# The first batch's product with v in the whole array with a column of ones, and an earlier pooling of q

## The chip, the cores and the metric

The kernel runs on one core of a Trainium2 chip. The metric is the device time of one execution in microseconds; it is the median of several runs. Five engines work side by side, each through its own queue of instructions in order: TensorE (PE in the rows: matrix products; its weight loads are PEld), VectorE (DVE), ScalarE (ACT), GpSimd (POOL), and SyncE (SP), which here issues all transfers (DMA).

## What is computed

```python
# attention: q, k, v are (batch 4, heads 8, 1152 positions, 64)
q_pool = q.reshape(B, H, S // 2, 2, D).mean(axis=3)          # 576 pooled queries
scores = scale * np.matmul(q_pool, k.transpose(0, 1, 3, 2))
scores = scores - np.max(scores, axis=-1, keepdims=True)
attn = np.exp(scores)
attn = attn / (np.sum(attn, axis=-1, keepdims=True) + 1e-09)
attn_out = np.matmul(attn, v)                                # to (2304 tokens, 512)
# two layers follow, (2304 x 512) by w_in (512 x 2048) and w_out (2048 x 512):
h = x @ w_in;  x = (h - np.tanh(h)) @ w_out                  # first layer
h = x @ w_in2; r = np.maximum(h, 0); x = (s*r*r + b) @ w_out2  # second layer
```

The weights of the layers arrive as 64-bit floats in two 32-bit words each, and are turned into pairs of 32-bit numbers on the chip.

## The kernel before

**Heads and tiles.** The 32 heads are worked off in 16 pairs (n = 0 to 15, four pairs for each of the four batches; the pair's heads are j = 0 and 1). One head has 9 tiles t of 128 keys. For a tile, `scores` makes the scores of 128 keys by 576 queries in two halves g of 288 queries, each by two products (L352 and L353), and ScalarE takes their exponential into a buffer pf (L354). The tile then waits in the list `pend` for its product with v.

**The product with v (tile pv).** `batch` takes three tiles at a time. v of a tile is 128 keys by 64, so that the product has 64 rows; the two halves g of the queries are put on the upper and the lower 64 rows of one PSUM tile, that is on two column tiles of the array that work side by side (L421, written 128*64 in the rows). Every product in plain 32 bits is two instructions in the trace (and one row in the order of instructions below); a head has 9 x 2 x 2 = 36 in the trace.

**The sum of a head's exponentials (tile su).** In the first batch (`plain`, n < 4) and for the very last head, `sum_plain` makes it on TensorE too: a product of 32 columns of ones with each pf (L387, 128*32), four column tiles side by side, again 36 in the trace for a head; after the head, ScalarE copies the result (sx, L394) and one product with `spread` (L396, tile pts) spreads it over 128 rows. From the second batch on, GpSimd adds up the pf of a head (`add`, L408, tile acc) and `total` makes one sum of them at the head's end (L434). `end` inverts the sum (tile ri, VectorE, L453); `store` multiplies it into the head's result (tile xv, copied from pv by L444), splits it on ScalarE and GpSimd (tile xo, L460), and `put` transfers it to DRAM (L464).

**Preparation.** `prep(n)` makes a pair's operands: it adds neighbouring q (tile qr, L265, on GpSimd for all pairs but the first), transposes q and k on TensorE (ptq L271, ptk L287), and makes the largest score of each query by a separate product (ptm, L312 to L316) that VectorE reduces (mp, L317; 27 a pair). VectorE and GpSimd also convert the first layer's weights in steps of seven instructions (tiles raw, t, w; L195 to L210), four steps in each pair of the first batch; a step reads raw, which a transfer fills (L178, L181), two steps ahead.

**Order.** The program is written by a clock of ticks, four for a tile. `prep(n + 2)` starts in the second head of pair n, at tile 9 - LEAD // 4, and goes on after so many ticks as its `yield`s say. Within TensorE's row of instructions a scheduler then orders by priority; `batch` is given a priority AHEAD = 400 and `prep`'s transposes SOON = 40. From pair 5 on, `fill` puts products of the first layer's first five slices for the batch before (tiles h, y: L487, L500) between the tiles; in the first pair of a batch (n = 4, 8, 12) there are none.

In PSUM, pv and su have one buffer each, pp (for ptm, ptq, ptk, pts) three, and the scores three.

Of the kernel before, what the change touches and what calls it, by code (L numbers as in the profile page):

```python
# [9 lines left out]
F32 = mybir.dt.float32  # L10
F32R = mybir.dt.float32r
I32 = mybir.dt.int32
AF = mybir.ActivationFunctionType
# [5 lines left out]
P = 128  # L19
# [5 lines left out]
LAG = 3  # L25
# [4 lines left out]
LAST_STEPS = 4  # L30


LEAD = 20
GAP = 30
GAP1 = 12
MAXSTEP = 2
# [20 lines left out]
def attention_moe_moe_kernel(  # L57
# [60 lines left out]
    for i in range(4):  # L118
        g = i % 2
        dve.memset(spread[32 * i:32 * i + 1, g * D:(g + 1) * D], 1.0)  # L120
    sb2 = cp.tile([P, 2], F32, name="sb2")

    NBH = B * 2
# [13 lines left out]
    def later(k, fn):  # L137
        queue.append((clock[0] + k, fn))
# [91 lines left out]
    kl = pp.tile([P, S], F32R, name="kl")  # L230
    qls = [pp.tile([P, SQ], F32R, name=f"ql{i}") for i in range(2)]
    cs = [pp.tile([NQS + 1 - j, P], F32R, name=f"c{j}") for j in range(2)]
    vos = [ap.tile([P, NKT, D], F32, name=f"vo{i}") for i in range(2)]
    U2 = [ap.tile([D + 1, SQ], F32R, name=f"U2_{j}") for j in range(2)]
    for j in range(2):
        dve.memset(f32(T2[j][D:D + 1, :]), 1.0)
# [15 lines left out]
    def v_of(n, j):  # L252
        b, hp = pairs[n]
        return v[b, 2 * hp + j].rearrange("(p t) d -> p t d", t=NKT)

    def prep(n):
# [5 lines left out]
        for j in range(2):  # L262
            eng = dve if n == 0 else pool
            with tc.issue_after(added[0].ins) if n > 1 else ExitStack():
                eng.tensor_add(qrs[0][:, :, j * D:(j + 1) * D], qrs[j][:, :, 0:D], qrs[j][:, :, D:2 * D])  # L265
        yield 4
        for g in range(2):
            with tc.high_priority(offset=SOON):
                pt = psP.tile([P, KB], F32, tag="pp", name=f"ptq{n}_{g}")
# [58 lines left out]
    def prep_head(n, j):  # L328

        ql = qls[n % 2]  # L330
        T1, U1 = ops[n]
        with tc.issue_after(moved[0].ins) if moved[0] else ExitStack():
            dma(out=f32(U2[j][0:D, :]), in_=f32(ql[j * D:(j + 1) * D, :]))
            dma(out=f32(T2[j][0:D, :]), in_=f32(T1[j][j * D:(j + 1) * D, :]))
            dma(out=vos[j], in_=v_of(n, j))
        yield 1
        while (n, j) not in maxes:
            yield 1
        u = U2[j][D:D + 1]
        q0 = j * QH  # L340
        dma(out=f32(u[:, q0:q0 + NQS * P].rearrange("o (a t) -> o a t", t=P)), in_=f32(cs[j][0:NQS, :]))
        q0 = (1 - j) * NQS * P
        dma(out=f32(u[:, q0:q0 + QH]), in_=f32(cs[0][NQS:NQS + 1, j * QH:(j + 1) * QH]))
        ready.add((n, j))

    def scores(n, j, t):
        T1, U1 = ops[n]
        pf = ap.tile([P, SQ], F32, tag="pf", name=f"pf{n}_{j}_{t}", bufs=PFB)
        for g in range(2):
            sl = slice(g * HB, (g + 1) * HB)  # L350
            ps = psS.tile([P, HB], F32, tag="s", name=f"s{n}_{j}_{t}_{g}")
            last[0] = mm(ps, T1[j][:, t * P:(t + 1) * P], U1[j][:, sl], start=True, stop=False)  # L352
            last[0] = mm(ps, T2[j][:, t * P:(t + 1) * P], U2[j][:, sl], start=False, stop=True)  # L353
            act(pf[:, sl], ps, AF.Exp, scale=SCALE)  # L354
            yield
        pend.append((n, j, t, pf))
        if plain(n, j):
            fresh.append((n, j, t, pf))
            return
        r = [t in x for x in GROUPS].index(True)  # L360
        if t == GROUPS[r][0]:
            accs[n, j, r] = pf
        else:
            later(SUM, lambda: add(n, j, t, r, pf))
        if t == NKT - 1:
            later(SUM, lambda: due.append((n, j)))

    def plain(n, j):

        return n < NPAIR or (n, j) == (len(pairs) - 1, 1)  # L370

    fresh = []
    sums = {}
# [29 lines left out]
    def add(n, j, t, r, pf):  # L403
# [3 lines left out]
            accs[n, j, r] = ap.tile([P, SQ], F32, tag="acc", name=f"acc{n}_{j}_{r}", bufs=4)  # L407
        added[0] = pool.tensor_add(accs[n, j, r], old, pf)  # L408

    def batch():  # L410


        todo = [pend.popleft() for _ in range(BATCH)]
        n, j, t, _ = todo[0]
        if t == 0:
            pvt[n, j] = psV.tile([P, HB], F32, tag="pv", name=f"pv{n}_{j}")
        po = pvt[n, j]
        with tc.high_priority(offset=AHEAD), tc.issue_after(last[0].ins):
            for i, (_, _, u, pf) in enumerate(reversed(todo)):
                for g in (1, 0):  # L420
                    mm(po[g * D:(g + 1) * D], vos[j][:, u], pf[:, g * HB:(g + 1) * HB],  # L421
                       start=(t == 0 and i == 0), stop=(u == NKT - BATCH))
            total()
            if plain(n, j):
                sum_plain(n, j, t)
        if t == NKT - BATCH:
            later(0, lambda: finish_head(n, j))

    def total():
        for n, j in due:  # L430
            su = psV.tile([P, HB], F32, tag="su", name=f"su{n}_{j}")
            for r in range(2):
                for g in (1, 0):
                    mm(su[g * D:(g + 1) * D], ones, accs[n, j, r][:, g * HB:(g + 1) * HB],  # L434
                       start=(r == 0), stop=(r == 1))
            later(0, lambda: end(n, j, su))
        due.clear()
# [109 lines left out]
    def tick():  # L547

        clock[0] += 1
        due = [x for x in queue if x[0] <= clock[0]]  # L550
        queue[:] = [x for x in queue if x[0] > clock[0]]
        for _, fn in due:
            fn()
        for p in list(preps):
            if p[1] <= clock[0]:
                try:
                    p[1] = clock[0] + next(p[0])
                except StopIteration:
                    preps.remove(p)
        if done[0] < total_ns - HOLD_NS:  # L560
            fill(MOE_NS / 4)
# [10 lines left out]
    for n in range(len(pairs)):  # L572
        b, hp = pairs[n]
        if n == 0:
            add_prep(1)
        for j in range(2):
            for t in range(NKT):
                if j == 1 and t == NKT - LEAD // 4 and n + 2 < len(pairs):
                    add_prep(n + 2)
                if t == LAG + 1:  # L580
                    if j == 1 and n + 1 < len(pairs):
                        preps.append([prep_head(n + 1, 0), clock[0]])
                    if j == 0 and n > 0:
                        preps.append([prep_head(n, 1), clock[0]])
                if hp == 1 and j == 0 and t == 0 and b > 0:
                    while moe:
                        fill(1000)
                    moe.extend(sweep1(b - 1, g) for g in range(2))
                while (n, j) not in ready:
                    tick()  # L590
                for _ in scores(n, j, t):
                    tick()
                tick()
                if len(pend) > BATCH:
                    batch()
                tick()
                if (n, j, t) in early1:
                    w1gen.step()
                if n == len(pairs) - 1 and (n, 1) in ready:
                    if FW not in slots:  # L600
                        pctx.close()
                        wpc = ctx.enter_context(tc.tile_pool(name="wc", bufs=1, reuse_waits="tile"))
                        new_slots(wpc, range(FW, FA))
                    w1gen.step()
# [192 lines left out]
```

## Time and profile before

| | us |
|---|---|
| median of 3 runs (lowest, highest) | 1429.94 (1429.66, 1430.97) |
| the profiled execution | 1429.16 |
| its span, from the first to the last instruction | 1427.4 |
| TensorE busy in the span | 1359.7 |
| VectorE busy | 865.0 |
| ScalarE busy | 559.6 |
| GpSimd busy | 385.5 |

The attention takes about the first 680 us, the first batch of it about the first 190. A busy TensorE is counted from an instruction's start to its modelled end, and instructions overlap: one that has been issued and waits behind another counts too. Times in the rows are microseconds from the span's start.

### The profile page before, as it was taken

To read this page: it belongs to the slowest core of one execution; us is meant where nothing else is said; L and a number is where in the kernel's file an instruction comes from. 1 tells how busy PE (TensorE), PEld (TensorE's weight loads), DVE (VectorE), ACT (ScalarE), POOL (GpSimd) and SP (SyncE) were. 2 spreads that over 40 slices of the span, in tenths; PEclk is the share of its full clock that TensorE was granted. 3 is DMA by queue.
4 is the path that set the end of the run, shared out by engine and by line. 5 is a ranking of instruction groups with operands and counts; after the bars stand their busy time and mean duration, and the time that the engine had idled before them with its cause. 6 is when DMAs were issued, how large, how long until landed. Compare 5 with 4: busy or idle time off the path is not lost.

```text
span 1427.4 us, 23107 instructions
## 1 busy us (share of the span) xinstructions
PE 1359.7 (95%) x8670; PEld 1157.2 (81%) x8670; DVE 865.0 (61%) x1640; ACT 559.6 (39%) x1360; POOL 385.5 (27%) x311
## 2 busy tenths in 40 slices
PE   5999898999999999998989998999999999999998
PEld 3666666777777777776989997999899989898997
DVE  7877785667566664759796399844963232323232
ACT  2544445555455544544332233333332222323232
POOL 1212136565556645654220033100210000000000
PEclk9999999999999999999999999999999999999999
DMA  8756655563546555344776134744602020201000
GB/s 196 172 145 160 163 135 139 127 170 92 149 111 164 128 145 143 88 109 139 236 237 220 34 132 158 230 133 147 206 30 67 0 67 0 67 23 44 1 23 23
DMA packets 157647, 169.62 MB, mean 119 GB/s; under 512 B 52064, under 2 KB 130016, under 8 KB 157536
## 3 DMA queue, kind: packets, MB, share of 16 engines
q1 hardware_dynamic: 157536, 168.15, 42.8%
q8 instruction: 68, 1.11, 0.3%
q14 instruction: 43, 0.35, 0.1%
HBM read 101.98 MB, written 30.67 MB: 93 GB/s over the span
## 4 chain that ended last, share of the span: by engine, by line
PE 72%; DVE 16%; DMA 5%; POOL 3%; issue 3%; ACT 1%; SPq 1%; DVEq 0%; POOLq 0%; ACTq 0%
PE h L662 19%; PE o L735 14%; PE pv L421 9%; PE ptm L316 5%; PE y L673 5%; PE s L352 4%; PE s L353 4%; PE y L500 3%; PE h L487 2%; DVE t L199 2%; DMA raw<-in_moe_w_out_dram 2%; DVE t L197 2%; DVE mp L317 2%; DVE t L195 2%; POOL acc L408 2%
## 5 line engine op out<-in xcount | busy, mean ns | idle before, releaser
L662 PE MATMUL h<-xx,w 128*128 128x288 f32 (+1 forms) x2328 | 388.1, 316 | 1.7 <-DVE thb L514 1.7
L662 PEld LDWEIGHTS h<-xx,w 128*128 128x128 f32 x2328 | 365.1, 189 | 11.0 <-DVE thb L514 2.6
L317 DVE TENSOR_REDUCE mp<-ptm 128x1 f32<-128x384 f32 x432 | 225.2, 549 | 128.7 <-PE ptm L316 118.9
L354 ACT ACTIVATE pf<-s 128x288 f32<-128x288 f32 x576 | 220.8, 410 | 125.1 <-PE s L353 117.6
L210 POOL TENSOR_TENSOR w<-t,w 128x512 fp32r<-128x512 f32 (+1 forms) x82 | 98.0, 1195 | 381.4 <-ACT w L209 281.5
L673 PE MATMUL y<-ghb,w 128*128 128x288 f32 x784 | 174.5, 297 | 11.8 <-DVE yr L681 7.8
L408 POOL TENSOR_TENSOR acc<-acc,pf 128x576 f32<-128x576 f32 x115 | 166.3, 1446 | 64.8 <-ACT pf L354 60.0
L735 PE MATMUL o<-w,g2h 128*128 128x512 f32 x576 | 180.6, 395 | 0.0
L352 PE MATMUL s<-U,T 128*128 128x288 f32 x576 | 177.2, 314 | 0.6
L353 PE MATMUL s<-U,T 65*128 65x288 f32 x576 | 173.4, 309 | 1.1 <-DMA U<-c 1.1
L421 PE MATMUL pv<-pf,vo 128*64 128x288 f32 x1152 | 165.0, 423 | 0.0
L316 PE MATMUL ptm<-T,U 128*128 128x384 f32 x384 | 141.6, 387 | 16.6 <-DVE mp L317 10.8
L755 DVE SCALAR_TENSOR_TENSOR r<-r,sb 128x384 f32<-128x384 f32 x96 | 60.1, 626 | 140.7 <-ACT r L754 140.7
L673 PEld LDWEIGHTS y<-ghb,w 128*128 128x128 f32 x784 | 132.7, 190 | 13.5 <-DVE yr L681 8.9
L760 DVE SCALAR_TENSOR_TENSOR g2l<-r,sb,g2h 128x384 fp32r<-128x384 f32 x96 | 59.5, 620 | 111.1 <-ACT g2h L759 111.0
L421 PEld LDWEIGHTS pv<-pf,vo 128*64 128x64 f32 x1152 | 75.6, 139 | 59.6 <-ACT pf L354 10.6
L352 PEld LDWEIGHTS s<-U,T 128*128 128x128 f32 x576 | 111.6, 194 | 14.4 <-ACT pf L354 6.8
L735 PEld LDWEIGHTS o<-w,g2h 128*128 128x128 f32 x576 | 107.3, 188 | 18.0
L673 PE MATMUL y<-glb,w 128*128 128x288 f32 x392 | 117.0, 298 | 4.8 <-DVE glb L518 4.7
L353 PEld LDWEIGHTS s<-U,T 65*128 65x128 f32 x576 | 111.6, 194 | 5.9 <-issue 4.5
L735 PE MATMUL o<-w,g2l 128*128 128x512 f32 x288 | 114.1, 396 | 0.0
L759 ACT ACTIVATE g2h<-r,sb 128x384 fp32r<-128x384 f32 x96 | 59.5, 620 | 125.4 <-PE o L735 110.1
(78 smaller groups left out, 1747.6 us busy)
## 6 DMA issues: line engine op xcount, KB each, us to landing
xx<-x1d SPq DMA_DIRECT2D x80, 288.0 KB, 4.9
T<-T SPq DMA_DIRECT2D x48, 288.0 KB, 4.7
raw<-in_moe_w_in_dram SPq DMA_DIRECT2D x23, 512.0 KB, 3.7
raw<-in_moe_w_out_dram SPq DMA_DIRECT2D x23, 512.0 KB, 4.2
qr<-in_q_dram SPq DMA_DIRECT2D x32, 288.0 KB, 3.2
kr<-in_k_dram SPq DMA_DIRECT2D x32, 288.0 KB, 4.4
T<-kl SPq DMA_DIRECT2D x32, 288.0 KB, 4.2
vo<-in_v_dram SPq DMA_DIRECT2D x32, 288.0 KB, 5.0
```

What stands on the lines that cost most here:

```text
L210: added[0] = pool.tensor_sub(w[:, 2 * i + 1, cols], x, f32(w[:, 2 * i, cols]))
L316: mm(pt, Uz[j][:, q0:q0 + P], T1[j][:, kk], start=True, stop=True)
L317: dve.reduce_max(mp[:, s, i:i + 1], pt, axis=AX.X)
L352: last[0] = mm(ps, T1[j][:, t * P:(t + 1) * P], U1[j][:, sl], start=True, stop=False)
L353: last[0] = mm(ps, T2[j][:, t * P:(t + 1) * P], U2[j][:, sl], start=False, stop=True)
L354: act(pf[:, sl], ps, AF.Exp, scale=SCALE)
L408: added[0] = pool.tensor_add(accs[n, j, r], old, pf)
L421: mm(po[g * D:(g + 1) * D], vos[j][:, u], pf[:, g * HB:(g + 1) * HB], start=(t == 0 and i == 0), stop=(u == NKT - BATCH))
L662: mm(ps[:, :n], w[:, a, c * P:(c + 1) * P], xx[:, c, x, 0:n], start=(i == 0 and c == 0), stop=(i == 2 and c == NDC - 1))
L673: mm(ys[i][c], w[:, a, c * P:(c + 1) * P], x, start=(f == fa and r == 0), stop=(f == fb - 1 and r == 2))
L735: mm(ys[i][r], x[:, r * P:(r + 1) * P], w[:, a], start=(f == 0 and n == 0), stop=(f == NFC - 1 and n == 2))
L755: dve.scalar_tensor_tensor(out=r, in0=r, scalar=sb2[:, 0:1], in1=r, op0=ALU.mult, op1=ALU.mult)
```

## The change

For the pairs of the first batch, v gets a 65th column of ones. The product of a tile and a half g is then 65 rows: 64 of the result and one that is the sum of the exponentials. The halves go to two PSUM tiles, which take the buffers pv and su, with the whole array for each; they are issued tile by tile, three tiles behind the scores, without the priority of `batch`. At the head's end ScalarE copies two sum rows and two results, and two products with `rows` (65 by 128, zero but for half a row of ones) spread the sums. All later pairs keep the column tiles of 64. LEAD goes from 20 to 32 ticks, and for n > 1 `prep` leaves 16 ticks in place of 4 between the addition of q and its transposes, so that only the addition moves, by three tiles.

```diff
-LEAD = 20
+LEAD = 32
...
+    rows = []
+    for g in range(2):
+        row = fp.tile([D + 1, P], F32, name=f"row{g}")
+        dve.memset(row, 0.0)
+        dve.memset(row[D:D + 1, g * D:(g + 1) * D], 1.0)
+        rows.append(row)
+    srow = fp.tile([D + 1, 2, HB], F32, name="srow")
+    dve.memset(srow, 0.0)
...
-    vos = [ap.tile([P, NKT, D], F32, name=f"vo{i}") for i in range(2)]
+    vos = [ap.tile([P, NKT, D + 1], F32, name=f"vo{i}") for i in range(2)]
+    for vo in vos:
+        dve.memset(vo[:, :, D:D + 1], 1.0)
...
-        yield 4
+        yield 4 if n < 2 else 16
...
-            dma(out=vos[j], in_=v_of(n, j))
+            dma(out=vos[j][:, :, 0:D], in_=v_of(n, j))
...
         pend.append((n, j, t, pf))
+        if n < NPAIR:
+            return
         if plain(n, j):
...
-        return n < NPAIR or (n, j) == (len(pairs) - 1, 1)
+        return (n, j) == (len(pairs) - 1, 1)
...
+    def single():
+
+        n, j, t, pf = pend.popleft()
+        if t == 0:
+            pvt[n, j] = [psV.tile([P, HB], F32, tag=x, name=f"{x}{n}_{j}") for x in ("pv", "su")]
+        po = pvt[n, j]
+        for g in range(2):
+            mm(po[g][0:D + 1], vos[j][:, t], pf[:, g * HB:(g + 1) * HB],
+               start=(t == 0), stop=(t == NKT - 1))
+            yield
+        if t == NKT - 1:
+            later(0, lambda: finish_single(n, j))
+
+    def finish_single(n, j):
+        xv = xvs[n, j] = fp.tile([P, HB], F32, tag="xv", name=f"xv{n}_{j}", bufs=3)
+        po = pvt.pop((n, j))
+        for g in range(2):
+            act(srow[D:D + 1, g], po[g][D:D + 1], AF.Copy)
+            act(xv[g * D:(g + 1) * D], po[g][0:D], AF.Copy)
+
+        def total():
+            pt = psP.tile([P, KB], F32, tag="pp", name=f"pts{n}_{j}")
+            for g in range(2):
+                mm(pt[:, :HB], rows[g], srow[:, g], start=(g == 0), stop=(g == 1))
+            end(n, j, pt[:, :HB])
+
+        later(2, total)
...
-                tick()
-                if len(pend) > BATCH:
-                    batch()
-                tick()
+                if pend[0][0] < NPAIR:
+                    if len(pend) > LAG:
+                        for _ in single():
+                            tick()
+                    else:
+                        tick()
+                        tick()
+                else:
+                    tick()
+                    if len(pend) > BATCH:
+                        batch()
+                    tick()
```

**TensorE's row in the first batch.** The first rows are of before, pair 1, first head, around its second batch of three tiles: the last scores, one sum ahead, six products with v, the other sums, and then the products for VectorE's maxima. In a row stand the line, the tile written, the tiles read, and the size.

```order
L353 MATMUL s_0_6_1_930<-U_0_163,T_0_139 128x288
L387 MATMUL su_0_943<-pf_0_0_776,ones 32x288
L421 MATMUL pv_0_878<-pf_0_5_909,vo_161 64x288 x2
L421 MATMUL pv_0_878<-pf_0_4_885,vo_161 64x288 x2
L421 MATMUL pv_0_878<-pf_0_3_867,vo_161 64x288 x2
L387 MATMUL su_0_943<-pf_0_0_776,ones 32x288
L387 MATMUL su_0_943<-pf_0_1_821,ones 32x288 x2
L387 MATMUL su_0_943<-pf_0_2_838,ones 32x288 x2
L387 MATMUL su_0_943<-pf_0_3_867,ones 32x288 x2
L387 MATMUL su_0_943<-pf_0_4_885,ones 32x288 x2
L387 MATMUL su_0_943<-pf_0_5_909,ones 32x288 x2
L321 MATMUL ptc_1_848<-ident,m_1_675 4x128
```

The same head in the changed kernel (L430 is the product with the column of ones, L327 the product for the maxima, L363 and L364 the scores):

```order
L363 MATMUL s_0_6_1_907<-U_1_0_157,T_1_0_151 128x288
L364 MATMUL s_0_6_1_907<-U_0_173,T_0_147 128x288
L430 MATMUL pv_0_845<-pf_0_3_829,vo_169 65x288
L327 MATMUL ptm_0_0_1_912<-T_2_0_153,U_2_0_159 128x384
L430 MATMUL su_0_846<-pf_0_3_829,vo_169 65x288
L363 MATMUL s_0_7_0_925<-U_1_0_157,T_1_0_151 128x288
L364 MATMUL s_0_7_0_925<-U_0_173,T_0_147 128x288
L327 MATMUL ptm_0_0_2_931<-T_2_0_153,U_2_0_159 128x384
L363 MATMUL s_0_7_1_934<-U_1_0_157,T_1_0_151 128x288
L364 MATMUL s_0_7_1_934<-U_0_173,T_0_147 128x288
L430 MATMUL pv_0_845<-pf_0_4_856,vo_169 65x288
```

What stood in one block of 18 products now stands as single products between the scores and the maxima.

**VectorE's row at the same head.** Before, around the conversion of weight slice 0's second half (raw_0_1; L195 to L207), with the maxima mp around it:

```order
L317 TENSOR_REDUCE mp_0_925<-ptm_0_2_1_1008 128x1
L195 TENSOR_SCALAR t_0_1_0_1359<-raw_0_1_0_1291 128x256
L197 SCALAR_TENSOR_TENSOR t_0_1_0_1359<-raw_0_1_0_1291,t_0_1_0_1359 128x256
L199 SCALAR_TENSOR_TENSOR t_0_1_0_1359<-raw_0_1_0_1291,t_0_1_0_1359 128x256
L202 TENSOR_SCALAR raw_0_1_0_1291<-raw_0_1_0_1291 128x256
L204 SCALAR_TENSOR_TENSOR t_0_1_0_1359<-raw_0_1_0_1291,t_0_1_0_1359 128x256
L207 CAST w_121<-t_0_1_0_1359 128x256
L195 TENSOR_SCALAR t_0_1_1_1414<-raw_0_1_1_1334 128x256
L197 SCALAR_TENSOR_TENSOR t_0_1_1_1414<-raw_0_1_1_1334,t_0_1_1_1414 128x256
L317 TENSOR_REDUCE mp_0_925<-ptm_0_2_2_1038 128x1
```

In the changed kernel, the steps of the same head's conversions (L204 to L216; L328 is the maximum):

```order
L328 TENSOR_REDUCE mp_0_902<-ptm_0_2_0_967 128x1
L204 TENSOR_SCALAR t_4_0_0_1204<-raw_4_0_0_889 128x256
L206 SCALAR_TENSOR_TENSOR t_4_0_0_1204<-raw_4_0_0_889,t_4_0_0_1204 128x256
L328 TENSOR_REDUCE mp_0_902<-ptm_0_2_1_975 128x1
L208 SCALAR_TENSOR_TENSOR t_4_0_0_1204<-raw_4_0_0_889,t_4_0_0_1204 128x256
L328 TENSOR_REDUCE mp_0_902<-ptm_0_2_2_984 128x1
L211 TENSOR_SCALAR raw_4_0_0_889<-raw_4_0_0_889 128x256
L204 TENSOR_SCALAR t_4_0_1_1247<-raw_4_0_1_938 128x256
L328 TENSOR_REDUCE mp_0_902<-ptm_0_3_0_994 128x1
L213 SCALAR_TENSOR_TENSOR t_4_0_0_1204<-raw_4_0_0_889,t_4_0_0_1204 128x256
L328 TENSOR_REDUCE mp_0_902<-ptm_0_3_1_1003 128x1
```

Conversions that stood eight in a row now alternate with maxima.

**GpSimd's row at the preparation of pair 6.** Before, in pair 4, where acc_0 belongs to its first and acc_1 to its second head:

```order
L408 TENSOR_TENSOR acc_0_1_2312<-acc_0_1_2312,pf_0_8_2330 128x576
L408 TENSOR_TENSOR acc_1_0_2393<-pf_1_0_2346,pf_1_1_2378 128x576
L408 TENSOR_TENSOR acc_1_0_2393<-acc_1_0_2393,pf_1_2_2395 128x576
L408 TENSOR_TENSOR acc_1_0_2393<-acc_1_0_2393,pf_1_3_2415 128x576
L265 TENSOR_TENSOR qr_153<-qr_153 96x6x64
L265 TENSOR_TENSOR qr_153<-qr_154 96x6x64
```

The same place in the changed kernel (L276 adds q, L421 adds the exponentials):

```order
L421 TENSOR_TENSOR acc_0_1_2192<-acc_0_1_2192,pf_0_8_2212 128x576
L276 TENSOR_TENSOR qr_161<-qr_161 96x6x64
L276 TENSOR_TENSOR qr_161<-qr_162 96x6x64
L421 TENSOR_TENSOR acc_1_0_2277<-pf_1_0_2228,pf_1_1_2260 128x576
L421 TENSOR_TENSOR acc_1_0_2277<-acc_1_0_2277,pf_1_2_2279 128x576
L421 TENSOR_TENSOR acc_1_0_2277<-acc_1_0_2277,pf_1_3_2299 128x576
```

The addition of q now stands ahead of the three additions of the second head.

## Rows read from the trace of the kernel before

**Rows 1.** The page's top line.

```profile
span 1427.4 us, 23107 instructions
```

**Rows 2.** By stretch: length; PE, PEld, DVE, ACT, POOL busy; granted clock; DMA; GB/s.

```profile
36.00:214.00 178.00, 165.98 (x1155) 111.10 (x1152) 140.79 (x314) 81.61 (x220) 41.73 (x44) 0.97 0.63 155
428.00:500.00 72.00, 71.97 (x495) 56.77 (x494) 47.36 (x83) 39.04 (x104) 44.04 (x35) 1.00 0.60 145
```

**Rows 3.** TensorE's timeline at a batch without sums: start, time, instruction, tile, count.

```profile
34.43 0.30 PE L353 MATMUL s<-U,T 65*128 65x288 f32 x1
34.66 1.68 PE L421 MATMUL pv<-pf,vo 128*64 128x288 f32 x12
36.27 0.40 PE L352 MATMUL s<-U,T 128*128 128x288 f32 x1
```

**Rows 4.** The same timeline at batches with sums.

```profile
38.59 1.68 PE L421 MATMUL pv<-pf,vo 128*64 128x288 f32 x12
40.20 1.66 PE L387 MATMUL su<-pf,ones 128*32 128x288 f32 x24
...
45.12 1.68 PE L421 MATMUL pv<-pf,vo 128*64 128x288 f32 x12
46.73 1.17 PE L387 MATMUL su<-pf,ones 128*32 128x288 f32 x12
```

**Rows 5.** The same timeline: a sum split off ahead, and the spreading product.

```profile
116.35 0.67 PE L387 MATMUL su<-pf,ones 128*32 128x288 f32 x2
...
113.52 0.65 PE L396 MATMUL pts<-sx,spread 128*128 128x288 f32 x2
```

**Rows 6.** Waits of TensorE in 36 to 214: who for whom, us, times, longest.

```profile
PE ptm L316 <- DVE mp L317: 9.3, 5, 2.9
PE ptc L321 <- DVE m L319: 1.2, 2, 1.0
PE s L353 <- DMA U<-c: 1.1, 1, 1.1
```

**Rows 7.** Waits of VectorE in the same stretch.

```profile
DVE mp L317 <- PE ptm L316: 15.5, 19, 2.3
DVE t L195 <- DMA raw<-in_moe_w_out_dram: 8.3, 4, 4.1
DVE t L195 <- DMA raw<-in_moe_w_in_dram: 5.1, 1, 5.1
```

**Rows 8.** A window, columns as in Rows 2, behind the wait at 67 us.

```profile
71.00:72.00 1.00, 1.00 (x6) 0.47 (x4) 0.92 (x3) 0.00 (x0) 0.00 (x0) 0.50 0.77 198
```

**Rows 9.** TensorE's timeline, a run of products for the maxima.

```profile
205.07 2.82 PE L316 MATMUL ptm<-T,U 128*128 128x384 f32 x7
```

**Rows 10.** Waits of TensorE for the addition of q, 213 to 643.

```profile
PE ptq L271 <- POOL qr L265: 9.0, 3, 3.5
```

**Rows 11.** GpSimd's timeline ahead of the first of them.

```profile
216.45 2.99 POOL L408 TENSOR_TENSOR acc<-acc,pf 128x576 f32<-128x576 f32 x2
219.40 2.05 POOL L265 TENSOR_TENSOR qr<-qr 96x384 f32<-96x384 f32 x2
```

**Rows 12.** TensorE's timeline at its end.

```profile
221.51 0.74 PE L271 MATMUL ptq<-ident,qr 96*128 96x96 f32 x3 [3.53 <-POOL qr L265]
```

**Rows 13.** Windows behind the three waits.

```profile
220.00:228.00 8.00, 6.49 (x32) 5.29 (x32) 2.49 (x5) 3.14 (x8) 4.59 (x5) 0.57 0.47 127
380.00:386.00 6.00, 5.66 (x32) 4.79 (x32) 1.97 (x4) 2.35 (x6) 3.28 (x4) 0.72 0.52 136
541.00:549.00 8.00, 6.99 (x33) 5.57 (x34) 1.99 (x4) 2.35 (x6) 4.48 (x4) 0.57 0.48 123
```

**Rows 14.** DMA issues from the page: size, us to landing.

```profile
kr<-in_k_dram SPq DMA_DIRECT2D x32, 288.0 KB, 4.4
vo<-in_v_dram SPq DMA_DIRECT2D x32, 288.0 KB, 5.0
```

**Rows 15.** ScalarE's copy of pv in 36 to 214, by line: busy, mean ns.

```profile
L444 ACT ACTIVATE xv<-pv 128x288 f32<-128x288 f32 x9 | 3.7, 411 | 8.9 <-PE pv L421 8.9
```

More of the change, by code (lines that the diff above doesn't have):

```diff
@@ L420, in batch @@
                 for g in (1, 0):
-                    mm(po[g * D:(g + 1) * D], vos[j][:, u], pf[:, g * HB:(g + 1) * HB],
+                    mm(po[g * D:(g + 1) * D], vos[j][:, u, 0:D], pf[:, g * HB:(g + 1) * HB],
                        start=(t == 0 and i == 0), stop=(u == NKT - BATCH))
```

## The prediction

> **What bounds the kernel now.** I read the windows by stretch first, then TensorE's timeline, then the waits. The span is 1427.4 us and the profiled execution 1429.16 us [rows 1], 0.8 us under the median of the runs; all sums below start from 1429.2. From the second batch on TensorE is the bound: in 428 to 500 it is busy 71.97 of 72 us at full clock [rows 2]. In the first batch it is busy 165.98 of 178 us and VectorE 140.79 [rows 2], and both are more tightly coupled than these shares say. TensorE waits for VectorE's maxima for 9.3 us in five waits, and 2.3 us more for a column of maxima and a transfer, together 11.6 us [rows 6]; VectorE in turn waits 15.5 us for products for the maxima, and 13.4 us for weights to convert [rows 7]. Each kind of wait makes the other: a block of products with v and sums holds TensorE for over 3 us, VectorE runs dry, and then a run of conversions that waits for its weights lets the three pp buffers fill up, and TensorE stands. After some of these waits the granted clock is 0.50 for a while, that is 1.2 of 2.4 GHz [rows 8]; over the stretch the mean is 0.97 [rows 2], so 0.03 of 178, 5.3 us of work, are lost to it. And "busy" hides some waiting: seven products for the maxima take 2.82 us [rows 9], 0.40 each, which is VectorE's pace; between scores one takes about 0.17.
>
> Elsewhere three waits stand out: the transposes of q wait 9.0 us for GpSimd's addition [rows 10]. The first of them shows why: two additions of exponentials from 216.45 on stand ahead of the addition of q, which runs from 219.40 to 221.45 [rows 11], and TensorE stands 3.53 us until 221.51 [rows 12]. The clock is lower after each of the three, 0.57, 0.72 and 0.57 on the mean of 8, 6 and 8 us [rows 13]. They fall in the first pair of the second, third and fourth batch, where no first-layer products stand between the tiles.
>
> **The product with v.** Removed, for each of eight heads: three batches. A batch without sums holds TensorE from the end of the last score product to the next one: start 34.43 plus 0.13 to 36.27 plus 0.10 that it still waits, 1.81 us for 12 products [rows 3]. With 24 sums it is 1.60 more of block, some 3.3 us with the entry; with 12 sums 1.1 more, 2.9 [rows 4]. The spreading product's two take 0.48 (0.65 less the drain of some 0.17) [rows 5]. That is 1.81 + 3.3 + 2.9 + 0.48 = 8.5 us a head. In six of the eight heads one sum stands ahead of the block, alone, and costs 0.6 [rows 5]. In all 8 x 8.5 + 6 x 0.6 = 71.6 us.
>
> Added for each head: 36 products of 65 rows and 4 for the spreading. The trace has no product with 65 stationary columns. The nearest row with the whole array is the spreading product: of the two in 0.65 us the second ends 0.24 after the first, since one alone lasts 0.41 [rows 5]. Two column tiles side by side go at the same pace: six pairs in 1.68 are 0.25 a pair [rows 3]. I take 0.24. Below, nothing speaks for less than half of it; above, 0.41 if each ran alone. So 40 x 0.24 x 8 = 76.8 us, and the work itself grows by **5.2 us**.
>
> A rule speaks against this part. The Trainium skill, TensorEngine Tiling (Array Packing), Overview, Theoretical Speedup, gives up to twice the speed where the smaller dimension is at most 64. Going by that alone, the 36 products with v take 8.64 where they took 4.32 of streaming, 34.6 us more for eight heads. The rows agree with the page on the products (0.24 for one against 0.25 for a pair), but they also show 2.7 us of sums a head that go, and the entries and drains around each block.
>
> **What the smoothing gives back.** The orders shown above put single products between scores and maxima, and VectorE's conversions alternate with maxima where eight stood in a row. So VectorE should rarely find three pp buffers full, and TensorE rarely stand. To be had are the 11.6 us of waits, the 5.3 of low clock, and some 6 of runs at VectorE's pace, an estimate: 2.82 less 7 x 0.17 is 1.6 us [rows 9], once in each of four pairs. That is 23 us. But the weights still arrive when their transfers do, and a late one still stops the maxima behind it; I take half, **11.3 us**. Bounds: nothing, and all of it.
>
> **Small things.** ScalarE makes four copies in place of two, each 0.41 [rows 15], 6.6 us in all, and was busy 81.61 of 178 [rows 2]. The next head's first product must wait for the copies of its half, since pv and su have one buffer; by the order four score products and some maxima stand between, about 0.9 us, against 0.4 to 0.8 of copies: nothing, at most 0.5 a head. VectorE's new fills of constants, about 1.3 us, lie at the start, where it then waits for weights anyway. v now lands in pieces of 64 numbers with a gap; k has always landed so, in 4.4 us against 5.0 [rows 14]: nothing.
>
> **The addition of q.** It moves ahead of the second head's additions on GpSimd, while the transposes keep their ticks. So four tiles lie between, some 8 us where tiles are shortest, against 2.05 us of addition. Queued behind it are additions of exponentials, whose sum is wanted only at the head's end. To be had: 9.0 us of waits, and 8 x 0.43 + 6 x 0.28 + 8 x 0.43 = 8.5 of clock, less some 0.7 that lies in the waits: 16.8 us. TensorE is dense on both sides of the waits, so nearly all of it should come: I take **15 us**, between 9 (the clock falls elsewhere) and 16.8.
>
> **Sum.** 1429.2 + 5.2 - 11.3 - 15 = **1408** us.
>
> **Rivals.**
> - *The first batch becomes purely TensorE's.* Everything named is recovered: 1429.2 + 5.2 - 23 - 16.8 = 1395. For it: VectorE has 140.79 of work in 178 and gets it evenly. Against: 13.4 us of waits for weights.
> - *Nothing comes back in the first batch.* TensorE goes on waiting for maxima behind late weights, now between singles: 1429.2 + 5.2 - 15 = 1419. For it: conversions stand at the same ticks, and SyncE's order of weight loads behind the puts is much the same.
> - *The addition of q is early and the wait only moves*, to the maxima or the sums, since the first pair of a batch has no other products to fill in: 1429.2 + 5.2 - 11.3 - 2 = 1421. Against: the rows after each wait are dense.
> - *A product of 65 rows is dearer* (the other side). If weight loads don't hide and each takes 0.41, 320 of them cost 54 us more: 1408 + 54 = 1462. It decides from (1429 - 1408) / 320 = 0.066 more, that is from 0.31 each. Against: the spreading product, with 128 stationary columns, goes at 0.24.
> - *The sums cost nothing before*, because they stood in time that TensorE would have waited anyway, so that their removal frees nothing: the product alone counts, 34.6 more, and with the 11.3 and 15 it ends at 1437.5. By the Trainium skill's page named above this is the expected direction. Against: 24 sums hold the array for 1.66 us of their own [rows 4].
>
> **How the numbers follow.** The forecast gets 0.50, and its own range is 1400 to 1416 (the clock, and half the smoothing by 6 us more or less). The full recovery gets 0.19, nothing in the first batch 0.15, the wait that moves 0.07, the dear product 0.05, the sums for nothing 0.04. The first four are all faster, 0.91; the tails of the second and third of these towards no change take some of it. 0.2% (2.9 us) is about what a measurement of this kernel can tell from no change: faster 0.86, within 0.05, slower 0.09. The range for 8 in 10 goes from 1393, beneath the full recovery, to 1422, above the wait that moves.
>
> **What the profile after would show.** Right: 288 products of 65 rows in the first batch, spaced 0.24 where two follow each other; no wait of TensorE for the addition of q and the clock near 1.00 at 216 to 228 and its like; TensorE's waits for maxima in the first batch about halved, and the fourth pair's last head finished some 6 us earlier than before. Wrong: products of 65 rows at more than 0.31; new waits of TensorE of about 3 us in the pairs 4, 8 and 12; waits of VectorE for weights as long as before with TensorE standing behind them; or waits of TensorE for ScalarE's copies at the heads' ends.

## The result, and the profile after

The changed kernel takes 1413.51 us (median of 4 runs, 1413.30 to 1415.52) against 1429.8 in the runs beside it: a ratio of 0.9895 [0.9875, 0.9915]. The forecast was 1408 with a range of 1393 to 1422. The total is 5.5 us off, but the experiments show that it came about otherwise than the sum said. The profiled execution took 1415.52 us.

The page's top line, the windows that answer to [rows 2], the waits of TensorE and VectorE in 36 to 214 that answer to [rows 6, 7], and TensorE's timeline at a tile, all of the kernel after:

```profile
span 1413.7 us, 22532 instructions
```

```profile
36.00:214.00 178.00, 176.17 (x980) 136.02 (x980) 141.34 (x308) 100.86 (x264) 49.60 (x51) 0.99 0.69 159
428.00:500.00 72.00, 71.90 (x495) 55.60 (x494) 45.75 (x83) 38.61 (x104) 44.57 (x35) 1.00 0.57 132
```

```profile
PE ptc L332 <- DVE m L330: 0.8, 1, 0.8
PE ptm L327 <- DVE mp L328: 0.8, 1, 0.8
...
DVE ri L494 <- ACT ri L491: 17.8, 5, 4.6
DVE mp L328 <- PE ptm L327: 15.6, 40, 1.1
...
DVE t L204 <- DMA raw<-in_moe_w_in_dram: 0.3, 1, 0.3
```

```profile
39.82 0.65 PE L430 MATMUL pv<-pf,vo 128*65 128x288 f32 x2
40.09 0.55 PE L327 MATMUL ptm<-T,U 128*128 128x384 f32 x1
40.48 0.65 PE L430 MATMUL su<-pf,vo 128*65 128x288 f32 x2
40.75 0.51 PE L363 MATMUL s<-U,T 128*128 128x288 f32 x1
...
41.68 0.65 PE L430 MATMUL pv<-pf,vo 128*65 128x288 f32 x2
```

In the first batch TensorE is now busy 176.17 of 178 us, where it was 165.98, and waits 1.6 us where it waited 11.6. The tile from 39.82 to 41.68 takes 1.86 us: four score products at 0.13, two for the maxima at 0.17, and 1.00 left for the four products with v, 0.25 each where 0.24 was taken. VectorE no longer waits for weights (0.3 us where it was 13.4), but it waits 17.8 us in five pieces for something that took 0.2 before: the reciprocal of a head's sum (ri) stands in its row at a place that it reaches before ScalarE has made the copy that it reads.

The addition of q answers to [rows 11, 13]. First GpSimd's timeline, where the addition (L276) now stands ahead of the second head's exponentials, then windows at the transposes of q, which now start at 206.4, 361.8 and 520.4:

```profile
195.18 2.91 POOL L421 TENSOR_TENSOR acc<-acc,pf 128x576 f32<-128x576 f32 x2
198.05 2.07 POOL L276 TENSOR_TENSOR qr<-qr 96x384 f32<-96x384 f32 x2
201.21 1.42 POOL L421 TENSOR_TENSOR acc<-pf,pf 128x576 f32<-128x576 f32 x1 [1.08 <-ACT pf L365]
```

```profile
203.00:213.00 10.00, 9.22 (x66) 7.16 (x63) 9.12 (x18) 5.50 (x16) 6.84 (x6) 1.00 0.59 151
364.00:374.00 10.00, 9.66 (x67) 7.72 (x67) 5.70 (x12) 6.65 (x18) 6.91 (x7) 1.00 0.81 205
523.00:533.00 10.00, 9.67 (x68) 7.59 (x68) 5.63 (x12) 6.91 (x18) 6.99 (x6) 1.00 0.85 211
```

No wait of TensorE for qr is left behind the first batch (it was 9.0 us, [rows 10]), and the granted clock is 1.00 at these places, where it was 0.57 and 0.72 [rows 13].

To see where time goes, the table compares when heads end. The end of a head is the start of ScalarE's split of its result (tile xo), read from ScalarE's timeline. Heads count from 1; the 9th is the first of the second batch. Each row of ends is one profiled execution. Up to the first head's end the kernel after and the one with the product only have the same instructions in the same order, and still end that head 1.1 us apart: a difference of about 1 us between two rows says nothing.

| kernel | median us | ratio, interval | 1st | 8th | 9th | 12th | 17th | 32nd |
|---|---|---|---|---|---|---|---|---|
| before | 1429.2 | | 54.5 | 202.3 | 216.7 | 280.0 | 375.6 | 677.9 |
| after | 1413.5 | 0.9895 [0.9875, 0.9915] | 60.5 | 193.9 | 204.5 | 266.2 | 364.6 | 658.4 |
| lead only | 1413.5 | 0.9887 [0.9864, 0.9910] | 54.3 | 199.5 | 216.1 | 270.7 | 365.9 | 658.2 |
| product only | 1430.3 | 1.0011 [0.9995, 1.0026] | 59.4 | 192.9 | 203.4 | 273.8 | 374.3 | 678.8 |
| blocks of three | 1418.0 | 0.9925 [0.9900, 0.9949] | 58.3 | 204.7 | 216.9 | 273.5 | 371.3 | 664.8 |
| before, v padded | 1432.9 | 1.0014 [0.9998, 1.0030] | 57.0 | 199.3 | 213.7 | 276.6 | 375.7 | 679.0 |
| v lands whole | 1415.9 | 0.9896 [0.9873, 0.9918] | 59.1 | 193.6 | 204.9 | 274.0 | 368.7 | 660.5 |
| constants on GpSimd | 1412.4 | 0.9874 [0.9851, 0.9896] | 58.7 | 192.2 | 202.7 | 264.5 | 362.8 | 656.0 |
| both of these | 1414.8 | 0.9891 [0.9868, 0.9914] | 56.5 | 190.4 | 201.7 | 272.0 | 366.7 | 658.7 |
| earlier steps | 1409.9 | 0.9865 [0.9839, 0.9891] | 59.2 | 194.9 | 205.4 | 263.5 | 361.2 | 654.1 |
| all steps early | 1408.8 | 0.9862 [0.9841, 0.9883] | 58.6 | 193.5 | 203.1 | 262.0 | 359.7 | 653.3 |
| earlier steps, constants | 1408.4 | 0.9859 [0.9836, 0.9881] | 58.1 | 193.7 | 204.3 | 262.4 | 360.1 | 653.1 |
| landing, constants, steps | 1407.3 | 0.9846 [0.9819, 0.9872] | 56.5 | 191.6 | 201.7 | 262.3 | 357.6 | 649.9 |

The ratios are against runs of the kernel before beside each kernel (medians 1427.7 to 1429.8). One kernel more, with column tiles one by one, follows below.

### The profile page after: what moved, and what is told of

The parts are those of the page before. It is cut to its first block, busy times and chain, and to the rows that moved or that the text cites. A ratio compares the mean times of both kernels' runs of the same rounds, so it can differ in the third digit from the quotient of the medians.

```text
span 1413.7 us, 22532 instructions
## 1 busy us (share of the span) xinstructions
PE 1353.6 (96%) x8398; PEld 1169.0 (83%) x8398; DVE 863.7 (61%) x1647; ACT 567.8 (40%) x1376; POOL 384.8 (27%) x311
## 4 chain that ended last, share of the span: by engine, by line
PE 77%; DVE 14%; DMA 4%; issue 2%; ACT 1%; POOL 1%; SPq 0%; DVEq 0%; ACTq 0%; POOLq 0%
PE h L711 20%; PE o L784 14%; PE pv L462 7%; PE y L722 5%; PE ptm L327 5%; PE s L363 5%; PE s L364 5%; PE y L541 3%; PE h L528 3%; PE pv L430 2%; DVE t L208 2%; PE su L430 2%; DVE t L206 2%; DMA raw<-in_moe_w_in_dram 2%; DVE t L204 2%
## 5 line engine op out<-in xcount | busy, mean ns | idle before, releaser
L328 DVE TENSOR_REDUCE mp<-ptm 128x1 f32<-128x384 f32 x432 | 229.2, 550 | 108.3 <-PE ptm L327 100.0
L722 PE MATMUL y<-ghb,w 128*128 128x288 f32 x784 | 175.2, 298 | 16.7 <-DVE yr L730 12.6
L363 PE MATMUL s<-U,T 128*128 128x288 f32 x576 | 184.6, 326 | 0.8 <-ACT pf L365 0.7
L421 POOL TENSOR_TENSOR acc<-acc,pf 128x576 f32<-128x576 f32 x115 | 166.3, 1446 | 66.5 <-ACT pf L365 61.4
L364 PE MATMUL s<-U,T 65*128 65x288 f32 x576 | 171.0, 305 | 0.0
L327 PE MATMUL ptm<-T,U 128*128 128x384 f32 x384 | 149.2, 400 | 9.4 <-DVE w L216 5.5
L363 PEld LDWEIGHTS s<-U,T 128*128 128x128 f32 x576 | 110.9, 192 | 13.5 <-ACT pf L365 4.2
L462 PE MATMUL pv<-pf,vo 128*64 128x288 f32 x864 | 120.7, 415 | 0.3 <-ACT pf L365 0.3
L364 PEld LDWEIGHTS s<-U,T 65*128 65x128 f32 x576 | 110.0, 192 | 7.0 <-issue 4.4
L803 ACT ACTIVATE r<-h 128x384 f32<-128x384 f32 x96 | 47.0, 489 | 143.9 <-PE h L711 143.3
```

The costliest lines, as they stand in the source:

```text
L327: mm(pt, Uz[j][:, q0:q0 + P], T1[j][:, kk], start=True, stop=True)
L328: dve.reduce_max(mp[:, s, i:i + 1], pt, axis=AX.X)
L462: mm(po[g * D:(g + 1) * D], vos[j][:, u, 0:D], pf[:, g * HB:(g + 1) * HB], start=(t == 0 and i == 0), stop=(u == NKT - BATCH))
L722: mm(ys[i][c], w[:, a, c * P:(c + 1) * P], x, start=(f == fa and r == 0), stop=(f == fb - 1 and r == 2))
```

## The experiments

**The two parts apart.** The kernel before with the lead alone:

```diff
-LEAD = 20
+LEAD = 32
...
-        yield 4
+        yield 4 if n < 2 else 16
```

> The kernel before with only the longer lead for the addition of q. Theory (the three waits and the low clock behind them are worth nearly all of the gain): TensorE's wait for the addition of q is gone, 1413 to 1417 us. Rival (the wait only moves, and the product with v brings the gain): 1422 to 1428 us, with new waits in pairs 4, 8 and 12.

The changed kernel with LEAD 20 and `yield 4`, so the product alone:

> The changed kernel with the old lead, so only the product in the whole array is new. Theory (the first batch gains some 5 us by its end, part of it lost elsewhere): 1424 to 1428 us, with the three waits for the addition of q back. Rival (the product brings most): 1413 to 1418 us.

The lead alone gives the whole gain, 1429.2 to 1413.46, and the product alone none, 1.0011; that misses both of its expectations. The heads' ends show that the second is no plain nothing. These are ScalarE's splits at the 1st, 9th, 17th and 32nd head, of the kernel after and of the kernel with the lead alone:

```profile
60.45 0.44 ACT L500 ACTIVATE xo<-xv 128x288 fp32r<-128x288 f32 x1
...
204.46 0.44 ACT L500 ACTIVATE xo<-xv 128x288 fp32r<-128x288 f32 x1 [1.68 <-DVE xv L499]
...
364.57 0.44 ACT L500 ACTIVATE xo<-xv 128x288 fp32r<-128x288 f32 x1 [1.57 <-DVE xv L499]
...
658.35 0.44 ACT L500 ACTIVATE xo<-xv 128x288 fp32r<-128x288 f32 x1
```

```profile
54.33 0.43 ACT L459 ACTIVATE xo<-xv 128x288 fp32r<-128x288 f32 x1
...
216.06 0.44 ACT L459 ACTIVATE xo<-xv 128x288 fp32r<-128x288 f32 x1 [1.69 <-DVE xv L458]
...
365.94 0.44 ACT L459 ACTIVATE xo<-xv 128x288 fp32r<-128x288 f32 x1 [0.47 <-DVE xv L458]
...
658.17 0.44 ACT L459 ACTIVATE xo<-xv 128x288 fp32r<-128x288 f32 x1
```

By stretch, after against lead only: 6.1 us later at the first head; then 144.0 against 161.7 to the ninth, 17.7 won; then 160.1 against 149.9 to the seventeenth, 10.2 lost; then 1.6 lost to the end. Four numbers, the largest 17.7, add up to 0.2.

Low clock stands in three of these four stretches. Toward the end of a wait of TensorE (1.83 us until 31.87 after, 2.82 until 90.19 with the lead alone) the granted clock falls to its lower level (0.50, 1.2 of 2.4 GHz) and stays there for almost 7 us; first after, then with the lead alone:

```profile
31.50:38.30 6.80, 6.43 (x27) 6.01 (x27) 3.58 (x8) 4.42 (x11) 0.00 (x0) 0.50 0.78 207
```

```profile
89.40:96.30 6.90, 6.11 (x22) 4.00 (x23) 4.31 (x8) 1.23 (x3) 0.00 (x0) 0.51 0.13 38
```

Two score products after one another start 0.24 us apart in the first of these windows (34.70, 34.94) and 0.13 behind it (41.41, 41.54). So 3.4 us of work are lost to it in each kernel, before the first head's end in the one and behind it in the other, and up to 3.4 us of the 6.1 lost and of the 17.7 won are the clock. After, a further stretch of it, 3.4 us, lies between the seventeenth head and the last. The 10.2 us lost in between hold none in either kernel.

**Is it the array or the order?** The changed kernel with the products of 65 rows three tiles at a time, with the priority of `batch`:

```diff
-                    if len(pend) > LAG:
-                        for _ in single():
-                            tick()
-                    else:
-                        tick()
-                        tick()
+                    tick()
+                    if len(pend) > BATCH:
+                        with tc.high_priority(offset=AHEAD), tc.issue_after(last[0].ins):
+                            for _ in range(BATCH):
+                                for _ in single():
+                                    pass
+                    tick()
```

> The changed kernel with the products of the first batch issued three tiles at a time with the old priority: the same work in blocks, all else equal. Theory (interleaving takes away the waits between TensorE and VectorE): the waits of some 10 us and the low clock come back, 1421 to 1428 us. Rival (the sums, entries and drains that went are the gain): within 2 us of the changed kernel, 1411 to 1416 us.

And the changed kernel with single tiles, but column tiles of 64 rows and sums in column tiles of 32 as before, each tile's products on their own:

> The changed kernel with column tiles of 64 and separate sums in the first batch, but tile by tile and without priority, as the change issues them. If interleaving alone is what helps: 1413 to 1420 us. If each change between whole array and column tiles costs what the blocks of before show (0.37 us for entry and exit, twice for each of 72 tiles, 53 us): 1440 to 1466 us.

Blocks of three take 1418.0 us, between their two expectations. In them the ninth head ends at 216.9, as with the lead alone: the whole array by itself wins nothing in the first batch, as the near balance of the terms (71.6 against 76.8) had it. Column tiles singly take 1467.3 us, 1.0263 [1.0237, 1.0289]. Their window of 36 to 214 shows TensorE never idle, with fewer products done than the 980 above:

```profile
36.00:214.00 178.00, 178.00 (x929) 86.82 (x925) 101.73 (x221) 64.23 (x175) 22.16 (x27) 1.00 0.50 114
```

54 us over 2 x 72 small blocks are 0.37 us for each, net of all else that differs between the two kernels. So the gain of the first batch needs both: single tiles to keep VectorE and TensorE even, and the whole array so that single tiles are cheap. The Trainium skill, TensorEngine Tiling (Array Packing), Overview, Theoretical Speedup, gives up to twice the speed for tiles of this size; used for one tile of keys at a time between other products, column tiles are the slower ones here. Why blocks of three lose 6.6 us by the last head against the lead alone was not followed up.

**The loss at the start.** The kernel before with v landing in padded rows, and nothing else:

```diff
-    vos = [ap.tile([P, NKT, D], F32, name=f"vo{i}") for i in range(2)]
+    vos = [ap.tile([P, NKT, D + 1], F32, name=f"vo{i}") for i in range(2)]
...
-            dma(out=vos[j], in_=v_of(n, j))
+            dma(out=vos[j][:, :, 0:D], in_=v_of(n, j))
```

> The kernel before with v landing in rows of 65 numbers, the 65th not used: only the landing of v differs. Theory (the small pieces fill the queue at the start and hold up the second pair's k): the issue of k takes some 5 us in place of 1.9, TensorE waits for k near 30 us, and the time is 2 to 5 us longer, 1431 to 1435 us. Rival (the landing is free, as forecast): within 1 us of before.

The changed kernel with v landing whole in a spare buffer, from which GpSimd copies it to the padded rows:

> The changed kernel with v landing whole; in the first batch GpSimd copies it into the rows of 65, later pairs use it as it lands. Theory (the landing in pieces costs at the start): k issues in about 1.9 us, no wait for k near 30 us, 1408 to 1411 us. Rival (it costs nothing, or the eight copies of about 1 us on GpSimd cost as much): 1412 to 1415 us.

The changed kernel with the new constants filled by GpSimd, and then both:

> The changed kernel with the new constants filled by GpSimd, not VectorE. Theory (VectorE's start is on the path: the first transposes came 1.1 us later than before): 1412 to 1413 us, first transposes at 6.1 us again. Rival (covered by the wait for the first weights): no change, 1413 to 1414 us.

> Both of the last two, v landing whole and the constants on GpSimd. If the costs add up: 1407 to 1410 us, and the fastest. If what the start gains is lost in the stage behind the attention, where TensorE waits for VectorE's copies of y: 1411 to 1414 us.

SyncE's timeline at the issue of the second pair's k, behind the first two loads of v, in the kernel before, after, before with v padded, and after with v landing whole:

```profile
21.83 1.89 SPq L250 DMA_DIRECT2D kr<-in_k_dram  x2
```

```profile
22.77 5.62 SPq L261 DMA_DIRECT2D kr<-in_k_dram  x2
```

```profile
23.02 4.21 SPq L250 DMA_DIRECT2D kr<-in_k_dram  x2
```

```profile
22.05 2.01 SPq L261 DMA_DIRECT2D kr<-in_k_dram  x2
```

The issue takes 4 to 6 us behind loads in pieces and 2 behind whole ones. After, TensorE waits for that k (1.83 us at 31.87). At the first head the landing is worth 1.4 us, the constants 1.8, both 4.0. Singly that is little more than the 1.1 us between equal rows. Both together win more than the sum, and the clock goes with it: it stands at its lower level for 6.8 us between 28 and 39 in the kernel after and with either part alone, and never there with both. In total time v padded in the kernel before is not clear of no change (1.0014 [0.9998, 1.0030]), and v landing whole takes 1415.9 us, above both of its expectations. And both together give no better time than the constants alone. The 3.5 us that they win by the eighth head are gone by the tenth (223.0 in both kernels), and by the twelfth the head is 5.8 late. TensorE's and VectorE's timelines of the kernel with both show where:

```profile
232.20 0.69 PE L327 MATMUL ptm<-T,U 128*128 128x384 f32 x1 [3.25 <-DVE mp L328]
```

```profile
223.33 1.66 DVE L206 SCALAR_TENSOR_TENSOR t<-raw,t 128x256 int32<-128x256 int32 x1
...
226.23 1.50 DVE L211 TENSOR_SCALAR raw<-raw 128x256 int32<-128x256 int32 x1
...
230.18 1.50 DVE L213 SCALAR_TENSOR_TENSOR t<-raw,t 128x256 f32<-128x256 int32 x1
```

Conversions of weights (t, raw) stand between VectorE's maxima at 223 to 232, in the second batch, and TensorE waits 3.25 us behind them. Its clock falls by the end of this wait, and within 1 us behind two others for VectorE (1.63 us until 207.96, 2.27 until 251.63), each time for 3.4 us, so that it is 0.93 on the mean from the ninth to the twelfth head, where it is 1.00 after:

```profile
201.70:272.00 70.30, 61.97 (x387) 47.39 (x386) 57.35 (x103) 32.48 (x88) 37.41 (x29) 0.93 0.52 127
```

That stretch is 8.6 us longer than after (61.7, its window stands below): 4.1 us more of idle time, and the rest is work at the lower clock.

**The steps that fell into the second batch.** Where conversions stand among the maxima (27 a pair) is seen in VectorE's row of instructions. Before, the first 26 conversions all stand ahead of the 134th maximum, and in the kernel with blocks of three ahead of the 133rd. After, the last five stand behind the 152nd, 156th, 174th, 177th and 182nd, that is behind the ninth head's end, by which 148 maxima have begun: with single tiles the scheduler placed them later. The table `CONVERT`, which says how many steps are written in each pair, moves them back:

```diff
-CONVERT = (4, 4, 4, 4, 2, 2, 0, 0, 0, 1, 1, 1, 1)
+CONVERT = (6, 6, 6, 2, 0, 0, 0, 0, 0, 1, 1, 1, 1)
```

> The changed kernel with one line changed: the weights' conversion steps of the pairs 0 to 5 stand at 6, 6, 6, 2, 0, 0 instead of 4, 4, 4, 4, 2, 2 places, so that in VectorE's row only two of the five steps stay behind the first batch (at the 152nd and 156th maximum, in place of the 152nd to 182nd). Theory A (the product part does win about 12 us by the first head of the second batch, 216.1 to 204.5, and loses them again because five steps, 35 instructions, fall into the second batch, where TensorE then waits about 5.5 us for maxima behind them and works some 2 us at their pace): the head that ends at 364.6 ends at 358 to 361, TensorE's waits for maxima between 200 and 380 fall from 3.9 to under 1.5 us, and the time is 1406 to 1410. Theory B (the 12 us were never there: work was only put off, and the second batch would take what it takes in any case): no change, 1412 to 1416. Theory C (the first batch has no room on VectorE, so that the steps moved there make TensorE wait there): the first batch ends 3 to 6 us later and the time is 1413 to 1419.

With (7, 7, 6, 0, 0, 0, ...):

> The same line at 7, 7, 6, 0, 0, 0: one step behind the first batch (at the 156th maximum), one at the 133rd. Theory A: a further 1 to 2 us below the kernel with two steps left, 1404 to 1409. Theory B: 1412 to 1416. Theory C: above the kernel with two steps left by 2 us or more, with new waits of TensorE for maxima or of VectorE for weights between 36 and 190.

With (6, 6, 6, 2, ...) and the constants on GpSimd:

> The steps at 6, 6, 6, 2 and the constants filled by GpSimd (which alone gave 1412.4, its heads 1.8 us earlier from the first to the last). Theory A with the two gains independent: 1404 to 1409, the shortest of all. Theory B: as with the constants alone, 1411 to 1414. Theory C: 1412 to 1418.

With (7, 7, 6, 0, ...), the constants on GpSimd and v landing whole:

> The kernel with v landing whole and the constants on GpSimd (1414.8; its first head 4.0 us earlier than in the changed kernel, 56.5 against 60.5, and its eighth 3.5, but its tenth and eleventh 0 and 5.8 later, where TensorE waits 3.3 us for maxima behind two conversions that take 1.5 us an instruction), now with the conversion steps at 7, 7, 6, 0, 0, 0. Theory A (whatever is won ahead of the second batch is lost in it behind the steps left there, and is kept once they are gone): the eighth head stays near 190, the last one ends at 649 to 651 against 658.7, and the time is 1404 to 1408, at or below every other kernel. Theory B (v landing whole costs in the second batch by itself, by GpSimd's additional copies and the later products): the tenth and eleventh head are late again without those steps, and the time is 1410 to 1415. Theory C (the first batch is full): its end moves from 190 to 193 or later, 1408 to 1411, as with the steps alone.

TensorE's waits in 200 to 380, first after, then with the steps at 7, 7, 6:

```profile
PE ptm L327 <- DVE mp L328: 2.9, 4, 1.1
PE y L541 <- DVE gla L559: 1.1, 1, 1.1
PE ptm L323 <- DVE mp L328: 1.0, 1, 1.0
PE h L528 <- DVE mp L328: 0.4, 1, 0.4
```

```profile
PE ptc L332 <- DVE m L330: 0.7, 1, 0.7
PE ptm L327 <- DVE mp L328: 0.6, 2, 0.4
PE s L363 <- ACT pf L365: 0.3, 1, 0.3
PE ptk L298 <- DVE mp L328: 0.2, 1, 0.2
```

The theory of the steps holds in all four: from the ninth to the seventeenth head it is 155.8 to 156.6 us where it was 160.1, the waits for maxima are nearly gone, the eighth head ends at most 1.5 us later than without the edit, and the times of the first three are 1409.9, 1408.8 and 1408.4. Their intervals overlap that of the change, though; it is the heads' ends that tell them apart. Against the same kernel with the old table the stretch from the ninth to the seventeenth head is 4.3, 3.5 and 4.3 us shorter, with no low clock in it in any of them. The last kernel settles the start as well: its last head ends at 649.9 (649 to 651 was expected), 8.8 us ahead of the same kernel with the old table (from the ninth to the seventeenth head 9.1 us are won, 5.1 of them the clock, which no longer falls there), and it takes 1407.26 us (1403.22 to 1409.86), 0.9846 [0.9819, 0.9872]. It beats both kernels.

What is lost against the lead alone between the ninth and the seventeenth head, 10.2 us after and still some 6 with the steps moved, is in part no loss. The windows from the ninth to the twelfth head, first after, then with the lead alone:

```profile
204.50:266.20 61.70, 57.43 (x393) 44.42 (x393) 54.26 (x103) 32.70 (x89) 38.53 (x31) 1.00 0.61 138
```

```profile
216.10:270.80 54.70, 54.09 (x376) 41.99 (x375) 36.15 (x67) 31.77 (x86) 35.73 (x27) 1.00 0.57 135
```

Of the 7.0 us between them 3.7 are idle time of TensorE (4.3 against 0.6), and 3.3 are work: 17 products more, nearly all because with single tiles TensorE had run less far ahead when the ninth head ended (342 products for scores, 166 for maxima and 36 transposes of q against 346, 170 and 42). So the 17.7 us of the first batch are some 14 when this is counted.

## Why the total was right and the sum was not

**The product's price, +5.2: right.** 288 products of 65 rows at some 0.25. The dear product, a rival, is out by that; and that the sums cost nothing before is out by the blocks of three, where the ninth head ends with the lead alone's and not 34.6 us later.

**The smoothing, -11.3: this term was mis-sized, and its reach was the step that failed.** In the first batch nearly everything named came back, as in the first rival: 17.7 us net are 22.9 with the 5.2 of work, or some 20 if only 14 are counted, against 23 named (half of which is 11.5, not 11.3). TensorE's waits for maxima fell to 0.8 us, not to half. But the sum stopped at the first batch's end. It said of VectorE that its conversions alternate with maxima instead of standing in rows; it did not ask where the last of them stand. They stand in the second batch, and there they cost TensorE 3.7 us of waits by the twelfth head alone. Moving them back won 3.5 to 4.3 us of that stretch (2.9 to 5.1 by the last head), so this cause is shown; with v landing whole it won 9.1, since there the clock fell behind the waits too. That the new wait of 17.8 us for the reciprocal adds to VectorE's lateness was not tried by itself.

**The small things, nothing: wrong by 6.1 us at the first head.** VectorE's new constants were put under waits for weights; but the first transposes wait for the addition of q behind them (7.2 us where it was 6.1, and 6.6 with the lead alone). v in small pieces was put level with k, which lands so too; its own landing was not the point, but the issue of the load behind it. Undoing both won back 4.0 us, the low clock among them; how much is due to each alone lies too near the scatter to say, and the 2.2 us that are left against the lead alone (56.5 against 54.3) were not explained. No product of TensorE waits for ScalarE's four copies; one weight load waits 0.2 us for one.

**The addition of q, -15: right.** By itself -15.7 (12.9 to 19.4 by the interval), with the waits gone and the clock at 1.00, as the steps said. In its profiled execution, the fastest of its six, 16.9 us are won between the eighth head and the last, the whole 16.8 that was named.

So -17.7 in the first batch, +6.1 at the start, +10.2 and +1.6 behind it leave 0.2, where the sum had 5.2 - 11.3 = -6.1; the lead gave what it should. The error of the total is nearly that 6.1, and the total lies inside the range because the lead's term carries it.

One of the signs came true by luck. The fourth pair's last head was to end some 6 us earlier than before; it ends 8.4 earlier, and 5.6 earlier than with the lead alone. Behind that stand two errors of opposite sign, a start 6.1 us later and some 12 us won after it.

**What stays open.** From the last head's end to the span's end it is 749.5 us before and 755.4 after; but also 749.1 with the lead alone, 755.1 with the product alone and 751.0 with the earlier steps. The granted clock costs there 6.2 us of work before and 6.8 after, but 1.8 with the lead alone, 9.7 with the product alone and 5.2 with the earlier steps: it makes up most of the difference to the lead alone and none of that to before. Each is one execution, and the time of a kernel varies by 2 to 11 us from run to run. TensorE waits there for VectorE's sums (yr) 7.8 us before and 12.6 after. Whether the change gives something back there was not settled.

## What to carry to other kernels

A stage that gets faster hands its neighbours' work on to the next stage: when TensorE was freed in the first batch, VectorE's background steps slid by a few places in its row, and they did their harm where nobody looked. So after a change look at where each background step of every engine now stands, and compare the ends of units of work stage by stage; a sum that comes out right in total can hide a gain and two losses of the same size. Where parts cancel, undo the losses one at a time, and again together: a gain ahead of a stage that VectorE paces shows only once that stage is free. And count with a wait the low clock behind it: in the kernel with both losses undone, three waits of 7.2 us together brought 5.1 more.

## What the runs showed of the hardware that was not expected

**Conversions beside GpSimd's additions.** After, a conversion of 0.28 us takes 1.46 where GpSimd adds exponentials at the same time; VectorE's and GpSimd's timelines, and TensorE's behind them:

```profile
208.05 1.46 DVE L204 TENSOR_SCALAR t<-raw 128x256 int32<-128x256 int32 x1
209.55 0.43 DVE L206 SCALAR_TENSOR_TENSOR t<-raw,t 128x256 int32<-128x256 int32 x1
...
210.55 0.55 DVE L328 TENSOR_REDUCE mp<-ptm 128x1 f32<-128x384 f32 x1
```

```profile
207.96 1.40 POOL L421 TENSOR_TENSOR acc<-pf,pf 128x576 f32<-128x576 f32 x1
```

```profile
211.16 0.44 PE L327 MATMUL ptm<-T,U 128*128 128x384 f32 x1 [0.78 <-DVE mp L328]
```

The conversion starts 0.09 us after the addition and ends 0.15 us after it. The Trainium skill, SBUF — State Buffer, SBUF: two separate sides, says that VectorE, in some of its instructions, and GpSimd share a pair of ports as an exclusive lock, which whichever starts first holds for its whole instruction; the rows agree. So a step moved from the first batch, where GpSimd adds no exponentials, into the second can cost more than its own time.

**A load in pieces holds up the next one's issue** (5.62 and 4.21 us against 1.89 and 2.01), though it moves the same 288 KB.
